# Turning pairs of bf16 as float32 words in the first stage of a recurrent-convolution and gated-unit gradient kernel

## The chip, the cores and the metric

The kernel runs on one core of a Trainium2 chip. The metric is the device time of one launch in microseconds (us). The engines are named as the profile does: PE is TensorE's matmul, PEld its weight load, DVE is VectorE, ACT is ScalarE, POOL is GpSimd, SP is SyncE, which here only issues DMAs.

## The reference

The function takes q, k, v (each 2048 rows of 1024, bf16), a four-tap filter shift_k, a long filter ssm_k (1024 channels of 2048 taps), a skip weight ssm_D, and three matrices w_gate, w_up (1024 x 3584) and w_down (3584 x 1024). It returns the output and the gradient of every input for a given grad_out.

```
xn = layernorm(q)
s  = xn * (long_conv(shift_conv(k) * v) + kv * ssm_D)     # long_conv by FFT of length 4096, kv = shift_conv(k) * v
h  = (xn @ w_gate) * (xn @ w_up)                          # 2048 x 3584
g  = silu(h @ w_down)
out = q + s * g
return out, grads of (q, k, v, shift_k, ssm_k, ssm_D, w_gate, w_up, w_down)
```

## The kernel before

**Stages.** The first stage (to about 513 us) computes the two products xn @ w_gate and xn @ w_up, forms h, and beside it runs the forward part of the long convolution. The second computes bm = h @ w_down and the gates (to about 710 us). The later ones compute the gradients; nothing of the change is in them but the names of a few views.

**The first stage on PE.** The 3584 columns are cut into 14 slabs of 256 columns of each of the two matrices (`load_slab`, tile `wslab`). A unit of work (`gu_unit`) takes one slab and four blocks of 128 rows (one, two or four blocks in the beginning). For each block eight matmuls of 512 columns sum over the 1024 channels: stationary is a 128x128 piece of the transposed normalized rows `XNT`, moving is the slab (L656). ACT copies the result to `gut` (L658), DVE forms `hN` = gate * up, POOL's queue stores it to `Hd`, and later the block is transposed ("turned") by PE to `hT`, since the second stage needs h with the 3584 columns in partitions. A turn is a matmul in transpose mode with the data as stationary operand and a 128x128 identity as moving operand; it goes to PSUM (tile `tr`), and ACT copies it out (L691). The turn of a unit is queued (`defer`) and done five blocks later (`flush(5)`).

The normalized rows are turned the same way, eight 128x128 pieces for a block of 128 rows, in `layer_norm` (L597, L608) and, for the last eight blocks, in `turn_late` (L617).

**The convolution.** Channels are worked in eight slices of 128 (`ds`). The transform of length 4096 over the rows is done as small DFTs: PE multiplies the rows of one residue (row number modulo 8) by tables of sines and cosines (`cmm`, L235), and DVE combines the residues (helper `tt` at L213 and `stt` at L284). There are two forms. With eight residues (`fwd8`) PE runs 16 matmuls of 256 columns and DVE combines more; with four (`fwd4_half`, `fwd4_sums`, `fwd4_outs`) PE runs 32 and DVE combines less. The list `EIGHT` names the pairs (slice, kind) that take the eight-residue form; kind 0 is the filter's spectrum in slices 1 to 7, kind 1 the data's (in slice 0 the other way round). The filter's 2048 taps of 128 channels are turned by `h_rows`: two blocks of eight turns (L752, L754), each of the elements 8 apart in a row.

**What sets the order.** The convolution is a generator that yields after each step with the step's cost on DVE in us, from which 0.95 of the PE time inside it (`pe_us`) is taken off (`net`). A planner (`make_pump`) lets it run so far that the costs done stand to their total `F_TOTAL` as the blocks of work done on PE stand to `NT` (225). The order that comes out is fixed on every engine. At the end of the stage PE goes on with matmuls of the second stage (`bm_first`, `late_mm`), and the four steps of the last inverse transform are put behind fixed ones of them:

```
    at = (52, 55, 58, 61)
    for n in range(at[3] + 1):
        mm = late_mm(n)
        if n in at:
            with tc.issue_after(mm.ins):
                step()
```

Of the kernel before, what the change touches and what calls it, by code (L numbers as in the profile page):

```python
# [10 lines left out]
ACT = mybir.ActivationFunctionType  # L11
ALU = mybir.AluOpType
AX = mybir.AxisListType
BF16 = mybir.dt.bfloat16
# [5 lines left out]
def build_kernel(  # L20
# [87 lines left out]
    KFd = dram.tile([8, P, 16, 256], BF16, name="KFd")  # L108
    DYFd = dram.tile([8, P, 16, 256], BF16, name="DYFd")
    GUd = dram.tile([NSL, 2, P, 2, 8, SLW], BF16, name="GUd")  # L110
    Hd = dram.tile([NSL, P, 2, NB, P], BF16, name="Hd")
    HTd = [[dram.tile([4, P, n, 256], BF16, name=f"HTd{i}{j}") for j, n in enumerate((8, 8, 8, 4))] for i in range(2)]
    DGd = dram.tile([NSL, 2, S, SLW], BF16, name="DGd")


    const = ctx.enter_context(tc.tile_pool(name="const", bufs=1))
    ident = const.tile([P, P], BF16, name="ident")
    make_identity(nc, ident[:])
    mhpi = const.tile([P, 1], F32, name="mhpi")
    nc.vector.memset(mhpi[:], -np.pi / 2)  # L120
    negpi = const.tile([P, 1], F32, name="negpi")
# [64 lines left out]
    def turn_tables(psp):  # L186

        for j in range(2):
            for rq in range(2):
                ps = psp.tile([P, 4, 2, P], BF16, name="psY")  # L190
                for i in range(4):
                    for k in range(2):
                        nc.tensor.transpose(ps[:, i, k, :], T4[j][:, 4 * rq + i, k, :], ident[:])
                nc.scalar.copy(out=TI[:, j, 4 * rq:4 * rq + 4], in_=ps[:])
                yield

# [15 lines left out]
    def tt(o, a, b, op):  # L212
        pinned(V.tensor_tensor(o, a, b, op))  # L213
# [315 lines left out]

    def keep_busy(n):  # L530
        for i in range(n):
            mm = nc.tensor.matmul(busy[:, i % 4, :], ident[:], ident[:], start=True, stop=True)
        return mm

    keep_busy(58)
# [11 lines left out]
    def load_slab(sl, eng):  # L547
        w = fw.tile([P, DC, 2, SLW], BF16, name="wslab")
        fs = slice(sl * SLW, (sl + 1) * SLW)
        for a, wsrc in ((0, B_w_up), (1, B_w_gate)):  # L550
            last = eng.dma_start(out=w[:, :, a, :], in_=wsrc[:, fs].rearrange("(dc p) f -> p dc f", p=P))
        return w, last

    def ln_load(b0, n, x4):
# [6 lines left out]

    tr_ln, act_copy = [None], [None]
    turn_rows = []

    def layer_norm(b0, n, x4):
        def small(name, dt=F32):
# [21 lines left out]
        for i in range(n):  # L588
            b = b0 + i
            q, qi = divmod(b, 4)  # L590
            last = V.tensor_scalar(x4[:, i, :], x4[:, i, :], mv[:, i, 0:1], RSTD[:, b:b + 1], op0=SUB, op1=MUL)
            if b < 2:
                for hh in range(2):
                    ps = ps_st.tile([P, 4, P], BF16, name="tr")
                    for dc in range(4):
                        d0 = (4 * hh + dc) * P
                        tr_ln[0] = nc.tensor.transpose(ps[:, dc, :], x4[:, i, d0:d0 + P], ident[:])  # L597
                    act_copy[0] = nc.scalar.copy(out=XNT[0][:, 4 * hh:4 * hh + 4, b * P:b * P + P], in_=ps[:])
                if b == 0:
                    with tc.issue_after(tr_ln[0].ins):  # L600
                        keep_busy(10)
                continue
            if b0 >= 8:
                turn_rows.append((x4[:, i, :], q, qi))
                continue
            ps = ps_st.tile([P, DC, P], BF16, name="tr")
            for dc in range(DC):
                tr_ln[0] = nc.tensor.transpose(ps[:, dc, :], x4[:, i, dc * P:(dc + 1) * P], ident[:])  # L608
            act_copy[0] = nc.scalar.copy(out=XNT[q][:, :, qi * P:(qi + 1) * P], in_=ps[:])
        c, r0 = divmod(b0, 8)  # L610
        return last, root, st(xnn[:, c, r0:r0 + n, :], x4[:, 0:n, :])

    def turn_late():
        for i, (x, q, qi) in enumerate(turn_rows):
            ps = ps_st.tile([P, DC, P], BF16, name="tr")
            for dc in range(DC):
                tr_ln[0] = nc.tensor.transpose(ps[:, dc, :], x[:, dc * P:(dc + 1) * P], ident[:])  # L617
            act_copy[0] = nc.scalar.copy(out=XNT[q][:, :, qi * P:(qi + 1) * P], in_=ps[:])
        turn_rows.clear()

    nop = lambda: None
# [18 lines left out]
    def gu_unit(sl, b0, n, w, tick):  # L640

        if n == 4:
            turn_of[0] += 1
            if turn_of[0] % 3 == 0 and sl < NSL - 2:
                gut = U[5][:, 2048:4096].rearrange("p (a i f) -> p a i f", a=2, i=4)
            else:
                gut = fg.tile([P, 2, 4, SLW], BF16, name="gut")
            hN = fg.tile([P, 2, 4, P], BF16, name="hN", bufs=3)
        else:
            gut = lnp.tile([P, 2, 2, SLW], BF16, name="gut_s", bufs=6)  # L650
            hN = lnp.tile([P, 2, 2, P], BF16, name="hN_s", bufs=6)
        for i in range(n):
            q, qi = divmod(b0 + i, 4)
            ps = ps_gu.tile([P, 512], F32, name="psg")
# [11 lines left out]

        def multiply():
            with tc.issue_after(last.ins) if b0 + n <= 4 and chunk[0] <= 2 else nullcontext():
                by_half = lambda t: t.rearrange("p i (a f) -> p a i f", a=2)
                tt(hN[:, :, 0:n], by_half(gut[:, 0, 0:n]), by_half(gut[:, 1, 0:n]), MUL)  # L670
            st(Hd[sl][:, :, b0:b0 + n, :], hN[:, :, 0:n])
            defer(turn)
        hn[0] = multiply

# [8 lines left out]

        def turn():
            hT = fg.tile([P, 2, 2, 2, P], BF16, name="hT") if chunk[0] > 5 else lnp.tile([P, 2, 2, 2, P], BF16, name="hT_s", bufs=5)
            ps = ps_tr.tile([P, 2, 2, 2, P], BF16, name="tr")
            for a in range(2):
                for i in range(n):
                    nc.tensor.transpose(ps[:, i // 2, a, i % 2, :], hN[:, a, i, :], ident[:])
            if n == 4:  # L690
                nc.scalar.copy(out=hT[:], in_=ps[:])  # L691
            else:
                nc.scalar.copy(out=hT[:, 0, :, 0:n], in_=ps[:, 0, :, 0:n])
            store(hT)

    h_out = []
    ht_st = [None]
    EIGHT = ((0, 0), (0, 1), (5, 0), (6, 0), (7, 0), (7, 1))
    INV8 = (2, 4, 5, 6, 7)
    SHIFT_W = 8 * 2.3  # L700

# [4 lines left out]
    def conv_forward():  # L706
# [36 lines left out]
        def h_rows(ds, c):  # L743
            if ds == 8:
                return
            hrow = S_["h", ds]
            if c == 0:
                S_["hx"] = cf.tile([P, NB, P], BF16, name="hx")
            pe_us[0] += 0.47
            ps = ps_tr.tile([P, 8, P], BF16, name="tr")  # L750
            with tc.issue_after(tr_ln[0].ins):
                nc.tensor.transpose(ps[:, 0, :], hrow[:, c, :, 0], ident[:])  # L752
            for r in range(1, 8):
                nc.tensor.transpose(ps[:, r, :], hrow[:, c, :, r], ident[:])  # L754
            nc.scalar.activation(S_["hx"][:, 8 * c:8 * c + 8, :], ps[:], ACT.Copy, scale=WSC)
            if c == 1:
                h_out.append(ds)
                if ds + 1 < 8:
                    load_h(ds + 1)
# [122 lines left out]
        cx.release()  # L882
        kst.release()

    F_TOTAL = 4 * SHIFT_W + 3.0 + 8 * (0.5 + FWD4_W + 1.3 + PROD_W + INV_W) + 10.0 - 0.95 * 8 * (4 * 1.75 + 0.95 + 4 * 0.9)
    F_TOTAL += len(EIGHT) * (FWD8_W - 9.6 + 0.95 * 1.75) - 2.0
    F_TOTAL += len(INV8) * (INV8_W - INV_W + 0.95 * 1.8)
    conv = conv_forward()
# [72 lines left out]
    slabs.append(w)  # L961

    def load_wd(j):
        return ld(WD[j], B_w_down[j * 512:(j + 1) * 512, :].rearrange("(c p) d -> p c d", p=P))

    def ht_rows(bp, f0, f1):
        assert f0 % 8 == 0 and f1 == min(f0 + 8, NF)
# [287 lines left out]
    def gate(b, ps, parts=None):  # L1255
# [23 lines left out]
        def turn():  # L1279
            ps = ps_tr.tile([P, DC, P], BF16, name=tr_name[0])  # L1280
            for dc in range(DC):
                nc.tensor.transpose(ps[:, dc, :], dbm[:, dc * P:(dc + 1) * P], ident[:])
            nc.scalar.copy(out=DBMT[b // 4][:, :, (b % 4) * P:(b % 4 + 1) * P], in_=ps[:])
        if b >= 12:
            defer(turn)
# [185 lines left out]
            next(others, None)  # L1471

    def load_h(sl):
        h = u8(HSL[sl % 3], "p (a b f) -> p a b f", a=2, b=NB)
        ld(h, Hd[sl])
        hs[sl] = h

# [60 lines left out]

    def dwd_mm(ps, h, f, dh):
        for b in range(NB):  # L1540
            nc.tensor.matmul(ps, h[:, f, b, :], DBM[b // 4][:, b % 4, dh * 512:(dh + 1) * 512],  # L1541
                             start=(b == 0), stop=(b == NB - 1))

    flush()
# [1 line left out]
    for k in range(NSL - 1):  # L1546
# [23 lines left out]
        for f in range(2):  # L1570
            if (k, f) == (12, 1):
                d_row = wo.tile([P, D], BF16, name="wbs")
                ps = ps_b.tile([P, 512], F32, name="psb")
                nc.tensor.matmul(ps[0:8, 0:P], ddo[:], ident[:], start=True, stop=True)
# [93 lines left out]
    for g in range(1, 4):  # L1668
        for b in (4 * g, 4 * g + 2):
            end = b == NB - 2  # L1670
            pss = [ps_x.tile([P, D], F32, name="psx") for i in range(2)]
            for n in range(12 if end else 14):
# [3 lines left out]
                    DBM[n] = u8((7, 0, 1, 9)[n], a=4)  # L1676
                    ld(DBM[n], DBMd[512 * n:512 * n + 512, :].rearrange("(b u) d -> u b d", u=P))
                if end and n == 4:
                    h = u8(2, "p (a b f) -> p a b f", a=2, b=NB)
# [87 lines left out]
```

## Time and profile before

| | us |
|---|---|
| three runs | 1917.39, 1917.96, 1918.56 |
| median | 1917.96 |
| span of the profiled execution | 1916.6 |
| PE busy | 1905.7 (99%) |
| DVE busy | 1557.1 (81%) |
| ACT busy | 640.0 (33%) |
| POOL busy | 334.5 (17%) |

The span runs from the first to the last instruction of one profiled execution, and the three timed runs took 0.8 to 2.0 us more than it. The granted clock of PE was 1.000 over the span. A row of a group of instructions reads: line, engine, operation, output<-inputs, shape, count | busy us, mean ns of one | idle time before them. A row in order of time reads: start, length, engine, line, operation, output<-inputs, count. The mean of a matmul is its latency; matmuls overlap, so the step from start to start is what one takes on PE.

### The profile page before, as it was taken

Reading aid. Unit: us, or ns where it says so; the run is one execution under the profiler, and the core shown is the slowest. Engines: PE = TensorE matmul, PEld = TensorE weight load, DVE = VectorE, ACT = ScalarE, POOL = GpSimd, SP = SyncE. Lnnn points to the kernel's source line nnn. Section 1 sums busy time; section 2 is a strip of 40 time slices with the busy share of each in tenths; the row PEclk is TensorE's granted clock in tenths of the full one; section 3 lists DMA queues with packets and bytes.
Section 4 is the critical chain, followed back from the end, with each engine's and each line's share of the span. In section 5 each row is a group of like instructions: output and inputs, shape, how many; then the busy total and the mean of one; then the engine's idle time right before and its main releaser. Section 6 shows DMA issues by size and latency. Waiting matters only on the chain. (4 is left out here: it accounts for less than half of the span.)

```text
span 1916.6 us, 27330 instructions
## 1 busy us (share of the span) xinstructions
PE 1905.7 (99%) x10915; PEld 1024.9 (53%) x10915; DVE 1557.1 (81%) x1723; ACT 640.0 (33%) x946; POOL 334.5 (17%) x465
## 2 busy tenths in 40 slices
PE   8999999999999999999999999999999999999999
PEld 5555555545544456666666665664444444444444
DVE  8999999999997556887999999999995205788862
ACT  5864555646433233432222222222222102011121
POOL 5121212111113220001031221111212101111120
PEclk9999999999999999999999999999999999999999
DMA  8776867668679997677887698585787999999962
GB/s 293 271 261 216 265 209 234 211 234 299 237 246 287 316 287 250 205 240 236 269 271 261 220 263 270 180 286 177 217 255 173 206 205 191 184 184 195 193 180 97
DMA packets 425487, 444.28 MB, mean 232 GB/s; under 512 B 268784, under 2 KB 343180, under 8 KB 410896
## 3 DMA queue, kind: packets, MB, share of 16 engines
q1 hardware_dynamic: 367888, 239.03, 46.9%
q0 software_dynamic: 41152, 174.15, 29.1%
q10 hardware_dynamic: 16320, 29.36, 4.1%
q8 instruction: 85, 1.39, 0.3%
q14 instruction: 42, 0.34, 0.1%
HBM read 193.87 MB, written 189.84 MB: 200 GB/s over the span
## 5 line engine op out<-in xcount | busy, mean ns | idle before, releaser
L656 PE MATMUL psg<-wslab,U 128*128 128x512 bf16 x1792 | 407.3, 379 | 3.0 <-DMA wslab<-in_B_w_gate_dram 2.0
L1458 PE MATMUL psb<-U,U 128*128 128x512 bf16 x1792 | 397.1, 379 | 0.0
L1603 PE MATMUL psx<-U,dgut 128*128 128x512 bf16 x1536 | 333.0, 379 | 0.5 <-DVE dxn L213 0.5
L1603 PEld LDWEIGHTS <-dgut 128*128 128x128 bf16 x1792 | 175.3, 98 | 212.1 <-issue 0.8
L1458 PEld LDWEIGHTS <-U 128*128 128x128 bf16 x1792 | 175.2, 98 | 198.0
L656 PEld LDWEIGHTS <-U 128*128 128x128 bf16 x1792 | 172.2, 98 | 187.4 <-issue 2.5
L1441 PE MATMUL psb<-wdt,U 128*128 128x256 bf16 x1792 | 205.6, 273 | 0.0
L213 DVE TENSOR_TENSOR W<-W 128x1024 f32<-128x1024 f32 (+1 forms) x192 | 189.1, 1001 | 4.2
L1441 PEld LDWEIGHTS <-U 128*128 128x128 bf16 x1792 | 175.3, 98 | 29.2
L1541 PE MATMUL psb<-U,U 128*128 128x512 bf16 x816 | 177.3, 379 | 0.0
L1463 ACT CAST wb<-psb 128x512 bf16<-128x512 f32 x112 | 65.6, 586 | 315.4 <-PE psb L1458 310.5
L1208 DVE SCALAR_TENSOR_TENSOR dkp<-dkT,kT 128x1024 bf16<-128x1024 bf16 (+2 forms) x64 | 78.3, 1224 | 104.0 <-DMA dkT<-DKSHd 102.2
L994 PE MATMUL psbm<-U,ht 128*128 128x512 bf16 x672 | 146.0, 379 | 0.0
L1541 PEld LDWEIGHTS <-U 128*128 128x128 bf16 x896 | 87.4, 98 | 104.3
L658 ACT CAST gut<-psg 128x512 bf16<-128x512 f32 x156 | 91.3, 588 | 120.0 <-PE psg L656 119.1
L1635 ACT ACTIVATE dx_t<-dxn 128x1024 bf16<-128x1024 f32 x15 | 15.9, 1057 | 324.2 <-DVE dxn L213 320.3
L994 PEld LDWEIGHTS <-ht 128*128 128x128 bf16 x672 | 65.6, 98 | 78.0
L213 DVE TENSOR_TENSOR U<-U,dht 128x2048 bf16<-128x2048 bf16 x56 | 68.3, 1221 | 46.4 <-ACT dht L1443 46.4
L1443 ACT CAST dht<-psb 128x512 bf16<-128x512 f32 x112 | 65.6, 587 | 116.3 <-PE psb L1441 116.3
L66 POOL DMA_DIRECT2D Hd<-hN x54 | 37.1, 686 | 292.3 <-DVE hN L213 289.4
L1582 ACT CAST wbs<-psb 128x512 bf16<-128x512 f32 x51 | 29.9, 586 | 145.4 <-PE psb L1541 137.3
L213 DVE TENSOR_TENSOR W<-SP 128x1024 f32<-128x1024 f32 x64 | 74.5, 1219 | 2.5 <-ACT SP L296 1.7
(261 smaller groups left out, 2386.3 us busy)
## 6 DMA issues: line engine op xcount, KB each, us to landing
U<-GUd SPq DMA_DIRECT2D x28, 1024.0 KB, 8.7
DGd<-U SPq DMA_DIRECT2D x28, 1024.0 KB, 6.5
GUd<-gut ACTq DMA_DIRECT2D x39, 512.0 KB, 5.5
out_dram<-wb SPq DMA_DIRECT2D x112, 128.0 KB, 4.8
U<-Hd SPq DMA_DIRECT2D x14, 1024.0 KB, 5.9
Hd<-hN POOLq DMA_DIRECT2D x54, 256.0 KB, 4.2
HTd<-hT SPq DMA_DIRECT2D x52, 256.0 KB, 3.9
ht<-HTd SPq DMA_DIRECT2D x18, 512.0 KB, 7.7
```

The lines of the kernel that those rows point to most:

```text
L66: ins = nc.gpsimd.dma_start(out=out, in_=in_)
L213: pinned(V.tensor_tensor(o, a, b, op))
L656: gu_mm[0] = nc.tensor.matmul(ps[:], XNT[q][:, dc, qi * P:(qi + 1) * P], w[:, dc].rearrange("p a f -> p (a f)"), start=(dc == 0), stop=(dc ...
L658: nc.scalar.copy(out=gut[:, :, i], in_=ps[:].rearrange("p (a f) -> p a f", a=2))
L994: mm = nc.tensor.matmul(ps[:, dh * 512:(dh + 1) * 512], ht(fc)[:, i * P:(i + 1) * P], WD[fc // 4][:, fc % 4, dh * 512:(dh + 1) * 512], sta ...
L1208: ins = V.scalar_tensor_tensor(prod[:].rearrange("p r d -> p (r d)")[:, lo:H], dkT[:, 0, lo:H], 1.0, kT[:, 0, 13 + m + lo:13 + m + H], op0 ...
L1441: nc.tensor.matmul(ps[:, x * SLW:(x + 1) * SLW], DBMT[2 * hf + g][:, dc, (b % 4) * P:(b % 4 + 1) * P], wdt[:, dc, :], start=(dc == 0), sto ...
L1443: nc.scalar.copy(out=dht[:, 2 * e:2 * e + 2].rearrange("p b f -> p (b f)"), in_=ps[:])
L1458: nc.tensor.matmul(ps[:], XN[b // 4][:, b % 4, dc * P:(dc + 1) * P], dgus[b // 8][:, :, b % 8], start=(b == 0), stop=(b == NB - 1))
L1463: nc.scalar.copy(out=wb[:, dc % 2].rearrange("p a f -> p (a f)"), in_=ps[:])
L1541: nc.tensor.matmul(ps, h[:, f, b, :], DBM[b // 4][:, b % 4, dh * 512:(dh + 1) * 512], start=(b == 0), stop=(b == NB - 1))
L1603: nc.tensor.matmul(ps[:, dh * 512:(dh + 1) * 512], t[n][:, f, i * P:(i + 1) * P], WGU[n][:, f, dh * 512:(dh + 1) * 512], start=(n == 0 and ...
```

## The change

A 32-bit word of two neighbouring bf16 is turned as one float32. One turn moves 128 rows of 128 words, which is 256 bf16 columns, to 128 partitions, and each partition then holds two bf16 rows interleaved; ACT's copy parts them. Half as many turns are issued for h (4 instead of 8 for four blocks), for the normalized rows and for the filter rows. Since a partition now holds neighbouring columns, other things follow that order: channel 8p + m instead of 128m + p for XNT and the slabs, the row pairs of w_down, and `Hd` in natural order. The identity becomes float32, and the bf16 identity is a view of every second half-word of it. Two entries of `EIGHT`, (5, 0) and (6, 0), go back to four residues. The planner's numbers follow.

```diff
-    Hd = dram.tile([NSL, P, 2, NB, P], BF16, name="Hd")
+    Hd = dram.tile([NSL, P, NB, SLW], BF16, name="Hd")
...
-    ident = const.tile([P, P], BF16, name="ident")
-    make_identity(nc, ident[:])
+    ident4 = const.tile([P, P], F32, name="ident4")
+    make_identity(nc, ident4[:])
+    ident = ident4[:].bitcast(BF16).rearrange("p (c j) -> p j c", j=2)[:, 1]
...
-            last = eng.dma_start(out=w[:, :, a, :], in_=wsrc[:, fs].rearrange("(dc p) f -> p dc f", p=P))
+            last = eng.dma_start(out=w[:, :, a, :], in_=wsrc[:, fs].rearrange("(p m) f -> p m f", m=DC))
...
+    def turn_x(x, q, qi, c0, n):
+
+        ps = ps_st.tile([P, n, P], F32, name="tr")
+        for c in range(n):
+            tr_ln[0] = nc.tensor.transpose(ps[:, c, :], x.bitcast(F32).rearrange("p (w i) -> p w i", i=4)[:, :, c0 + c], ident4[:])
+        act_copy[0] = nc.scalar.copy(out=XNT[q][:, 2 * c0:2 * (c0 + n), qi * P:(qi + 1) * P].rearrange("p (c j) s -> p c j s", j=2),
+                                     in_=ps[:].bitcast(BF16).rearrange("p c (s j) -> p c j s", j=2))
...
                 for hh in range(2):
-                    ps = ps_st.tile([P, 4, P], BF16, name="tr")
-                    for dc in range(4):
-                        d0 = (4 * hh + dc) * P
-                        tr_ln[0] = nc.tensor.transpose(ps[:, dc, :], x4[:, i, d0:d0 + P], ident[:])
-                    act_copy[0] = nc.scalar.copy(out=XNT[0][:, 4 * hh:4 * hh + 4, b * P:b * P + P], in_=ps[:])
+                    turn_x(x4[:, i], 0, b, 2 * hh, 2)
...
-            ps = ps_st.tile([P, DC, P], BF16, name="tr")
-            for dc in range(DC):
-                tr_ln[0] = nc.tensor.transpose(ps[:, dc, :], x4[:, i, dc * P:(dc + 1) * P], ident[:])
-            act_copy[0] = nc.scalar.copy(out=XNT[q][:, :, qi * P:(qi + 1) * P], in_=ps[:])
+            turn_x(x4[:, i], q, qi, 0, 4)
...
-                by_half = lambda t: t.rearrange("p i (a f) -> p a i f", a=2)
-                tt(hN[:, :, 0:n], by_half(gut[:, 0, 0:n]), by_half(gut[:, 1, 0:n]), MUL)
-            st(Hd[sl][:, :, b0:b0 + n, :], hN[:, :, 0:n])
+                tt(hN[:, 0:n], gut[:, 0, 0:n], gut[:, 1, 0:n], MUL)
+            st(Hd[sl][:, b0:b0 + n, :], hN[:, 0:n])
...
-            ps = ps_tr.tile([P, 2, 2, 2, P], BF16, name="tr")
-            for a in range(2):
-                for i in range(n):
-                    nc.tensor.transpose(ps[:, i // 2, a, i % 2, :], hN[:, a, i, :], ident[:])
+            ps = ps_tr.tile([P, 2, 2, P], F32, name="tr")
+            for i in range(n):
+                nc.tensor.transpose(ps[:, i // 2, i % 2, :], hN[:, i, :].bitcast(F32), ident4[:])
+            halves = ps[:].rearrange("f q i s -> f q (i s)").bitcast(BF16).rearrange("f q (i s a) -> f q a i s", i=2, a=2)
             if n == 4:
-                nc.scalar.copy(out=hT[:], in_=ps[:])
+                nc.scalar.copy(out=hT[:], in_=halves)
...
-    EIGHT = ((0, 0), (0, 1), (5, 0), (6, 0), (7, 0), (7, 1))
+    EIGHT = ((0, 0), (0, 1), (7, 0), (7, 1))
...
-            pe_us[0] += 0.47
-            ps = ps_tr.tile([P, 8, P], BF16, name="tr")
+            pe_us[0] += 0.25
+            ps = ps_tr.tile([P, 4, P], F32, name="tr")
+            pairs = hrow[:, c].rearrange("p u r -> p (u r)").bitcast(F32).rearrange("p (u i) -> p u i", i=4)
             with tc.issue_after(tr_ln[0].ins):
-                nc.tensor.transpose(ps[:, 0, :], hrow[:, c, :, 0], ident[:])
-            for r in range(1, 8):
-                nc.tensor.transpose(ps[:, r, :], hrow[:, c, :, r], ident[:])
-            nc.scalar.activation(S_["hx"][:, 8 * c:8 * c + 8, :], ps[:], ACT.Copy, scale=WSC)
+                nc.tensor.transpose(ps[:, 0, :], pairs[:, :, 0], ident4[:])
+            for i in range(1, 4):
+                nc.tensor.transpose(ps[:, i, :], pairs[:, :, i], ident4[:])
+            nc.scalar.activation(S_["hx"][:, 8 * c:8 * c + 8, :].rearrange("u (i j) d -> u i j d", j=2),
+                                 ps[:].bitcast(BF16).rearrange("u i (d j) -> u i j d", j=2), ACT.Copy, scale=WSC)
...
-    F_TOTAL = 4 * SHIFT_W + 3.0 + 8 * (0.5 + FWD4_W + 1.3 + PROD_W + INV_W) + 10.0 - 0.95 * 8 * (4 * 1.75 + 0.95 + 4 * 0.9)
+    F_TOTAL = 4 * SHIFT_W + 3.0 + 8 * (0.5 + FWD4_W + 1.3 + PROD_W + INV_W) + 10.0 - 0.95 * 8 * (4 * 1.75 + 0.5 + 4 * 0.9)
...
-        return ld(WD[j], B_w_down[j * 512:(j + 1) * 512, :].rearrange("(c p) d -> p c d", p=P))
+        return ld(WD[j].rearrange("p (s a) d -> p s a d", a=2), B_w_down[j * 512:(j + 1) * 512, :].rearrange("(s p a) d -> p s a d", s=2, a=2))
...
-            nc.tensor.matmul(ps, h[:, f, b, :], DBM[b // 4][:, b % 4, dh * 512:(dh + 1) * 512],
+            nc.tensor.matmul(ps, h[:, b, f * P:(f + 1) * P], DBM[b // 4][:, b % 4, dh * 512:(dh + 1) * 512],
```

The uses of the identity that stay bf16 (the tables, the rows of dbm, PE's warm-up in `keep_busy`) take the view.

More of the change, by code (lines that the diff above doesn't have):

```diff
@@ L192, in turn_tables @@
                     for k in range(2):
-                        nc.tensor.transpose(ps[:, i, k, :], T4[j][:, 4 * rq + i, k, :], ident[:])
+                        nc.tensor.transpose(ps[:, i, k, :], T4[j][:, 4 * rq + i, k, :], ident)
                 nc.scalar.copy(out=TI[:, j, 4 * rq:4 * rq + 4], in_=ps[:])
@@ L531, in keep_busy @@
         for i in range(n):
-            mm = nc.tensor.matmul(busy[:, i % 4, :], ident[:], ident[:], start=True, stop=True)
+            mm = nc.tensor.matmul(busy[:, i % 4, :], ident, ident, start=True, stop=True)
         return mm
@@ L613, in turn_late @@
     def turn_late():
[L614 to L618, printed above, removed]
+        for x, q, qi in turn_rows:
+            turn_x(x, q, qi, 0, 4)
         turn_rows.clear()
@@ L647, in gu_unit @@
                 gut = fg.tile([P, 2, 4, SLW], BF16, name="gut")
-            hN = fg.tile([P, 2, 4, P], BF16, name="hN", bufs=3)
+            hN = fg.tile([P, 4, SLW], BF16, name="hN", bufs=3)
         else:
             gut = lnp.tile([P, 2, 2, SLW], BF16, name="gut_s", bufs=6)
-            hN = lnp.tile([P, 2, 2, P], BF16, name="hN_s", bufs=6)
+            hN = lnp.tile([P, 2, SLW], BF16, name="hN_s", bufs=6)
         for i in range(n):
@@ L685, in turn @@
             hT = fg.tile([P, 2, 2, 2, P], BF16, name="hT") if chunk[0] > 5 else lnp.tile([P, 2, 2, 2, P], BF16, name="hT_s", bufs=5)
-            ps = ps_tr.tile([P, 2, 2, 2, P], BF16, name="tr")
-            for a in range(2):
-                for i in range(n):
-                    nc.tensor.transpose(ps[:, i // 2, a, i % 2, :], hN[:, a, i, :], ident[:])
+            ps = ps_tr.tile([P, 2, 2, P], F32, name="tr")
+            for i in range(n):
+                nc.tensor.transpose(ps[:, i // 2, i % 2, :], hN[:, i, :].bitcast(F32), ident4[:])
+            halves = ps[:].rearrange("f q i s -> f q (i s)").bitcast(BF16).rearrange("f q (i s a) -> f q a i s", i=2, a=2)
             if n == 4:
-                nc.scalar.copy(out=hT[:], in_=ps[:])
+                nc.scalar.copy(out=hT[:], in_=halves)
             else:
-                nc.scalar.copy(out=hT[:, 0, :, 0:n], in_=ps[:, 0, :, 0:n])
+                nc.scalar.copy(out=hT[:, 0, :, 0:n], in_=halves[:, 0, :, 0:n])
             store(hT)
@@ L1281, in turn @@
             for dc in range(DC):
-                nc.tensor.transpose(ps[:, dc, :], dbm[:, dc * P:(dc + 1) * P], ident[:])
+                nc.tensor.transpose(ps[:, dc, :], dbm[:, dc * P:(dc + 1) * P], ident)
             nc.scalar.copy(out=DBMT[b // 4][:, :, (b % 4) * P:(b % 4 + 1) * P], in_=ps[:])
@@ L1473, in load_h @@
     def load_h(sl):
-        h = u8(HSL[sl % 3], "p (a b f) -> p a b f", a=2, b=NB)
+        h = u8(HSL[sl % 3], "p (b f) -> p b f", b=NB)
         ld(h, Hd[sl])
@@ L1573, in build_kernel @@
                 ps = ps_b.tile([P, 512], F32, name="psb")
-                nc.tensor.matmul(ps[0:8, 0:P], ddo[:], ident[:], start=True, stop=True)
+                nc.tensor.matmul(ps[0:8, 0:P], ddo[:], ident, start=True, stop=True)
                 nc.scalar.copy(out=d_row[0:8, 0:P], in_=ps[0:8, 0:P])
@@ L1678, in build_kernel @@
                 if end and n == 4:
-                    h = u8(2, "p (a b f) -> p a b f", a=2, b=NB)
+                    h = u8(2, "p (b f) -> p b f", b=NB)
                     ld(h, Hd[NSL - 1])
```

## The prediction

> **What bounds the kernel now.** I read the page's table of engines first, then the busy time by stretches of 48 us, then who waited for whom, then the order of time at the places that the change touches.
>
> ```profile
> PE 1905.7 (99%) x10915; PEld 1024.9 (53%) x10915; DVE 1557.1 (81%) x1723; ACT 640.0 (33%) x946; POOL 334.5 (17%) x465
> ...
> DVE  8999999999997556887999999999995205788862
> ```
> The first line says that TensorE (PE) works all the time: 1916.6 - 1905.7 leaves 10.9 us of idle time in the whole span. The second says that VectorE (DVE) is as full as PE in the first 12 slices (to 575 us). The change lies inside that stretch. The answer by stretches (columns: window, its length, then busy us and instructions of PE, PEld, DVE, ACT, POOL):
>
> ```profile
> 96.00:144.00 48.00, 47.91 (x318) 28.09 (x315) 47.55 (x49) 29.40 (x40) 11.98 (x17) 1.00 0.79 260
> ...
> 624.00:672.00 48.00, 48.00 (x224) 21.80 (x223) 25.18 (x40) 12.06 (x12) 10.17 (x16) 1.00 1.08 315
> ```
> In the first stage PE and DVE are both full; afterwards PE alone. The list of waits agrees: PE waited 6.5 us in the whole span, all but 0.5 of it in the first 50 us. So a microsecond taken from PE in the first stage is worth a microsecond only if DVE gives one up too, or has room. How much room it has is seen where the stage ends: PE runs matmuls of the next stage (psbm) until the last inverse transform (psY<-HX) needs what DVE finishes last (HX, L284). In order of time, PE then DVE:
>
> ```profile
> 550.78 5.99 PE L994 MATMUL psbm<-U,U 128*128 128x512 bf16 x27
> 556.61 0.60 PE L446 MATMUL psY<-HX,TI 128*128 128x256 bf16 x4
> ...
> 552.59 2.49 DVE L284 SCALAR_TENSOR_TENSOR HX<-W 128x512 bf16<-128x512 f32 x4
> ```
> DVE is done at 552.59 + 2.49 = 555.1, PE asks at 556.6. DVE has 1.5 us of room at this join, and at the last turn of h some 0.5 us (hN ready at 512.4, its matmul at 513.2, held by the copy of the turn before).
>
> **What the transposes cost now.** The groups by line give their counts:
>
> ```profile
> L689 PE MATMUL tr<-ident,hN 128*128 128x128 bf16 x432 | 33.1, 219 | 0.1
> ...
> L754 PE MATMUL tr<-ident,U 128*128 128x128 bf16 x112 | 9.6, 226 | 0.0
> ...
> L689 PEld LDWEIGHTS <-hN 128*128 128x128 bf16 x432 | 28.7, 98 | 12.1 <-issue 0.3
> ...
> L754 PEld LDWEIGHTS <-U 128*128 128x128 bf16 x112 | 8.2, 147 | 3.0 <-issue 2.8
> ```
> The mean of 219 ns is a latency, not a price, as matmuls overlap. The price is the step from one start to the next, read from the order of time:
>
> ```profile
> 206.19 0.22 PE L752 MATMUL tr<-ident,U 128*128 128x128 bf16 x1
> 206.25 0.60 PE L754 MATMUL tr<-ident,U 128*128 128x128 bf16 x7
> 206.69 1.04 PE L457 MATMUL psY<-HX,TI 128*128 128x256 bf16 x8
> ...
> 208.46 1.67 PE L656 MATMUL psg<-wslab,U 128*128 128x512 bf16 x7
> 209.97 0.61 PE L689 MATMUL tr<-ident,hN 128*128 128x128 bf16 x8
> 210.41 0.81 PE L656 MATMUL psg<-wslab,U 128*128 128x512 bf16 x3
> ```
> Eight turns of h hold PE from 209.97 to 210.41: 0.44 us, 55 ns each. Eight of the filter rows, whose elements lie 16 bytes apart in SBUF, take 206.19 to 206.69: 62.5 ns each; their weight loads are the slower ones (147 against 98 ns). Normalized rows, 32 turns at 25.67 in 1.99 us: (1.99 - 0.22) / 31 = 57 ns. The same reading gives (1.67 - 0.38) / 6 = 215 to 216 ns for a 512-column matmul and, from the 16 forward-transform matmuls that took 1.91 us at 226.85, (1.91 - 0.27) / 15 = 109 ns for one of 256 columns.
>
> **The change, part by part.** *Removed:* 448 turns of h (432 + 16 in the smaller tile hN_s) x 55 ns = 24.6 us; 128 of normalized rows (16 + 16 + 32 + 64 at L597, L608, L617) x 57 = 7.3; 128 of filter rows (112 + 16) x 62.5 = 8.0. Together 39.9 us of PE.
>
> *Added:* half as many, 352, each of 128x128 float32. No row of this trace has a float32 operand on PE, so I bound one. Below: 55 ns, the bf16 turn, if only the count of columns matters. Above: 216 ns, the 512-column row, if four bytes make four passes. I take 62.5 ns, because the nearest row is the filter's: there the load already fetches 128 elements one by one with no two neighbours together, which is the most a float32 load of 128 words must do, and the matmul behind it still streams 128 columns. 352 x 62.5 = 22.0 us. The filter and normalized rows keep a 16-byte pitch, the h rows become contiguous words.
>
> The Trainium skill speaks against this: "TensorE: Matmul & The Clock Gate", sections "LDWEIGHTS (loading the stationary operand)" and "Weight-path perf modes — Fast Weight Load (FWL) and DoubleRow", says that the fast weight load is off for FP32 and that a plain load takes columns / 1.2 ns, 107 ns for 128 columns. The sum by the page would be, as an estimate, 352 x 107 = 37.7 us added. No row here shows a plain load of 128 columns, so the trace neither agrees nor disagrees.
>
> *Two transforms back to four residues* (the filter spectra of slices 5 and 6): each needs 32 instead of 16 matmuls of 256 columns, so 32 x 109 ns = 3.5 us more on PE. On DVE they get shorter. From the order of time: the eight-residue one of slice 6 runs from 434.87 to 451.39, less 0.60 for an hN product inside, 15.9 us; the four-residue one at 374.16 to 383.96, less 0.61, 9.2 us. Two save 13.4 us. ACT copies the same four SP tiles either way.
>
> *The sum.* PE: 39.9 - 22.0 - 3.5 = 14.4 us less. DVE: 13.4 us less, plus its 1.5 us of room, plus what it gains at the beginning, where it waited 0.9 us for the last turn at L617 and 1.7 us for an SP copy, both behind PE. So DVE allows 14.9 to 17.5 us, PE's 14.4 binds, narrowly. The planner's total F_TOTAL falls by 15.5 of 441 (3.4 up for the turns, 18.9 down for the two transforms) and is spread over the same 225 ticks, so both engines thin out along the whole stage, though PE's gain is even and DVE's falls on two slices. Before slice 5 PE can be a few us ahead; hN products have five units (5 x 8 x 216 ns = 8.6 us) between product and turn to take that up.
>
> *Copies behind the turns.* ACT reads 1024 halves interleaved in words instead of 1024 in a row. Rows near it: 1.02 us for 1024 bf16 (L691) and 1.03 for 1024 float32 (L296): the count decides, so I take 1.02. If it doubled, filter blocks, which follow one another through one PSUM buffer, would wait 1 us in each of 8 pairs: 8 us; below, nothing.
>
> *Costed at nothing.* The h product keeps 1024 elements (0.68 us, as contiguous gate products have). The h store becomes half as many, longer pieces; POOL is 5 to 13 us busy in 48 and h is not read back before 1253.8. Wd pieces grow from 2 to 4 KB; slab pieces stay 512 bytes. A slab is asked for a whole slab ahead (some 35 us of PE), and its two halves land after 5.4 and 8.1 us; were that cover gone, a wait like the 1.0 us at the start would come 12 times. The float32 identity is written by POOL before PE's warm-up, and read with a stride by it; I put 0.3 us (0 to 1) there, of which the wait for the first slab (1.0 us at 9.3) hides some. Nothing waits anew elsewhere: both engines enter the second stage earlier by about the same, where DVE has 23 us idle in 48.
>
> So about 14 us come off the span: 1916.6 - 14.0 = 1902.6. The three runs took 0.8 to 2.0 us more than the profiled span, their median 1917.96 is 1.4 above it; **forecast 1904.0 us**.
>
> **Rivals.** *A, the plain load binds:* if a float32 weight is fed as two bf16 wide, a turn lasts like 256 columns, 109 ns. Then 352 x 109 = 38.4, PE: 39.9 - 38.4 - 3.5 = 2.0 us more, 1920. Against it: the slowed load of the filter rows (147 ns) still let the stream go at 62.5. For it: in that row only the pitch was bad, not the width. By the skill's 107 ns the estimate is 1.3 us more, no change that could be seen.
>
> *B, several passes (the other side):* each turn streams its columns more than twice, at L689, L754 and turn_x. At four passes, 216 ns, 352 x 216 = 76.0, so 39.9 - 76.0 - 3.5 = 39.6 us more: 1957.6. It breaks even at (39.9 - 3.5) / 352 = 103 ns and is slower by over 0.2% from 114 ns. For it: twice the bytes per column and no float32 matmul in this trace. Against it: a turn moves words, it does not need the product split. The skill's page ("Terms") says that transpose mode makes FP32 four times faster on this chip, which would exclude it; no run shown so far bears that out.
>
> *C, DVE caps it:* at 55 ns PE would save 39.9 - 19.4 - 3.5 = 17.0 us and DVE's 14.9 to 17.5 decides: 1901 to 1903.
>
> *D, half the gain:* 80 ns each (28.2 us, 8.2 saved), or the copies doubled (14 - 8 = 6 saved): 1910 to 1912.
>
> **How the numbers follow.** Chances: forecast and C together 0.56, D 0.10, A 0.14, B and anything past 114 ns 0.20. A difference below 0.2% (3.8 us) is about what a measurement of this kernel can't tell from no change. So faster 0.66 (forecast, C, D), same 0.14 (A), slower 0.20. The range runs from C's 1901 to just past A, 1922, which leaves out B's far part, below 2 in 10. The likeliest case alone: 1901 to 1907.
>
> **What would show it.** Right: 352 float32 turns, with 4 of h between two 512-column matmuls in about 0.25 us (0.44 in A, 0.86 in B); the psY<-HX matmul of the join at about 542.5, with no PE wait above 1 us there; DVE's L284 group smaller by 8 instructions; L691 near 1.02 us; the stage after unchanged in length. Wrong: a step above 100 ns between turns, PE waiting for DVE at L446 or L689, or ACT's copies near 2 us.

## The result and the profile after

The changed kernel took 1920.75 us in the median (20 runs, 1920.53 to 1923.23), the kernel before 1917.75 in the same comparison (20 runs). The ratio is 1.0016, 95% interval 1.0009 to 1.0022: 3.0 us longer, inside the 0.2% that the prediction counted as no change, though the interval lies above 1. The forecast was 1904.0. The span of the profiled execution is 1919.1 us (1916.6 before), the granted clock of PE 1.0.

The page of the changed kernel, its table of engines and DVE's row of 40 slices:

```profile
PE 1902.0 (99%) x10465; PEld 1029.3 (54%) x10595; DVE 1544.8 (80%) x1699; ACT 640.0 (33%) x946; POOL 327.0 (17%) x465
...
DVE  8999999999987555887899999999996205788862
```

The 10595 weight loads are the planned count: 10915 - 352 + 32. (130 matmul records are missing from this trace, so PE's busy time reads a little low.) DVE gave up 12.3 us. Its 9s now end one slice earlier, but the stage did not get shorter. By stretches of the changed kernel (window, length, busy us and instructions of PE, PEld, DVE, ACT, POOL):

```profile
96.00:144.00 48.00, 47.74 (x278) 27.87 (x283) 47.45 (x49) 28.79 (x39) 11.83 (x18) 1.00 0.77 259
...
432.00:480.00 48.00, 47.44 (x270) 27.28 (x274) 44.77 (x45) 28.51 (x41) 4.94 (x8) 1.00 0.84 286
...
624.00:672.00 48.00, 47.79 (x220) 21.79 (x223) 25.53 (x40) 11.72 (x13) 10.18 (x16) 1.00 1.06 299
```

PE is as full as before in each. DVE has 3 us idle at 432 to 480, where slices 5 and 6 were meant to free it. The same is seen at the join of the stages, in order of time, PE then DVE:

```profile
559.84 0.60 PE L447 MATMUL psY<-HX,TI 128*128 128x256 bf16 x4
...
551.12 2.50 DVE L285 SCALAR_TENSOR_TENSOR HX<-W 128x512 bf16<-128x512 f32 x4
```

DVE is done at 553.6, PE asks at 559.8. DVE's room grew from 1.5 to 6.2 us, and PE came 3.2 us later instead of 14 us earlier. The stage after has its old length: its successor (psb<-wdt, L1441) starts at 709.29, 3.25 later than before.

So it is PE, and the term to look at is the float32 turn. Groups of the changed kernel, then order of time:

```profile
L686 PE MATMUL tr<-ident,hN 128*128 128x128 f32 x216 | 32.7, 273 | 0.2
...
L753 PE MATMUL tr<-ident,U 128*128 128x128 f32 x48 | 8.4, 284 | 0.0
...
L686 PEld LDWEIGHTS tr<-ident,hN 128*128 128x128 f32 x216 | 26.8, 141 | 10.7 <-ACT hT L689 0.8
...
L753 PEld LDWEIGHTS tr<-ident,U 128*128 128x128 f32 x48 | 7.2, 209 | 0.2
```

```profile
200.81 0.60 PE L686 MATMUL tr<-ident,hN 128*128 128x128 f32 x4
201.24 0.38 PE L236 MATMUL psF<-hx,TF 128*128 128x256 bf16 x2
...
211.52 0.52 PE L753 MATMUL tr<-ident,U 128*128 128x128 f32 x3
211.88 1.04 PE L458 MATMUL psY<-HX,TI 128*128 128x256 bf16 x8
...
25.96 2.20 PE L570 MATMUL tr<-ident,U 128*128 128x128 f32 x16 [0.92 <-DVE U L600]
```

Four turns of h hold PE from 200.81 to 201.24: 0.43 / 4 = 108 ns each. The last three of four filter turns take 211.52 to 211.88, 120 ns each. Sixteen of normalized rows, also of words 16 bytes apart, take (2.20 - 0.28) / 15 = 128 ns each. Half as many turns at twice the step give nothing back. The latencies (273 and 284 ns) are close to the 272 of a 256-column bf16 matmul, not to the 219 of the bf16 turn.

### The profile page after: what moved, and what is told of

It reads as the page before. It is cut to its first block, busy times and chain, and to the rows that moved or that the text cites. A ratio compares the mean times of both kernels' runs of the same rounds, so it can differ in the third digit from the quotient of the medians.

```text
span 1919.1 us, 26552 instructions
## 1 busy us (share of the span) xinstructions
PE 1902.0 (99%) x10465; PEld 1029.3 (54%) x10595; DVE 1544.8 (80%) x1699; ACT 640.0 (33%) x946; POOL 327.0 (17%) x465
## 4 chain that ended last, share of the span: by engine, by line
PE 97%; ACT 1%; issue 1%; DVE 1%; DMA 1%; SPq 0%; ACTq 0%
PE psb L1458 20%; PE psx L1603 20%; PE psg L655 19%; PE psb L1441 10%; PE psbm L994 10%; PE psb L1541 9%; PE psF L236 3%; PE tr L686 1%; PE psY L447 1%; PE psY L1152 1%; PE psx L1541 1%; DMA wslab<-in_B_w_gate_dram 1%; PE psY L458 0%; PE tr L570 0%; ACT SP L258 0%
## 5 line engine op out<-in xcount | busy, mean ns | idle before, releaser
L655 PE MATMUL psg<-wslab,U 128*128 128x512 bf16 x1738 | 401.5, 379 | 6.1 <-DMA wslab<-in_B_w_gate_dram 2.6
L1441 PE MATMUL psb<-wdt,U 128*128 128x256 bf16 x1792 | 205.6, 273 | 0.0
L1441 PEld LDWEIGHTS <-U 128*128 128x128 bf16 x1792 | 175.3, 98 | 29.2
L214 DVE TENSOR_TENSOR W<-W 128x1024 f32<-128x1024 f32 (+1 forms) x186 | 184.0, 1006 | 4.1
L66 POOL DMA_DIRECT2D Hd<-hN x54 | 30.3, 562 | 296.0 <-DVE hN L214 283.3
```

Of the source, the lines that this page charges most:

```text
L655: gu_mm[0] = nc.tensor.matmul(ps[:], XNT[q][:, dc, qi * P:(qi + 1) * P], w[:, dc].rearrange("p a f -> p (a f)"), start=(dc == 0), stop=(dc ...
L1441: nc.tensor.matmul(ps[:, x * SLW:(x + 1) * SLW], DBMT[2 * hf + g][:, dc, (b % 4) * P:(b % 4 + 1) * P], wdt[:, dc, :], start=(dc == 0), sto ...
```

## The experiments

**1. The step of a turn by itself (steps).** Ten rows of 32 matmuls behind the warm-up of the changed kernel, whose output stays as it is. They differ in type, pitch and width; a row's first operand is stationary, its second moving, and the data in `Dz` are zeros. The kernel took 1952.97 us (one run), 32 us more than the changed kernel where some 25 were expected; only its rows are read.

```diff
+    for i in range(N):
+        nc.tensor.transpose(bh[:, i % 8, :], Dz[:, 0:128], ident)
...
+    for i in range(N):
+        nc.tensor.transpose(bh[0:127, i % 8, :], Dz[:, 0:127], ident)
...
+    for i in range(N):
+        nc.tensor.transpose(busy[:, i % 4, :], Dz[:, 0:256].bitcast(F32), ident4[:])
...
+    for i in range(N):
+        nc.tensor.transpose(busy[:, i % 4, :], fw_[:, :, i % 4], ident4[:])
...
+    for i in range(N):
+        nc.tensor.transpose(busy[0:64, i % 4, :], Dz[:, 0:128].bitcast(F32), ident4[:])
...
+    for i in range(N):
+        nc.tensor.transpose(busy[:, i % 4, 0:64], Dz[0:64, 0:256].bitcast(F32), ident4[0:64, 0:64])
```

> The changed kernel with ten rows of 32 matmuls put behind the warm-up, each row with its own line, four 512-column matmuls between rows; their output is not used, and the kernel is some 25 us longer for them. Read is the step from start to start in each row. Two theories of what makes a float32 turn take 109 ns contiguous and 128 ns at a 16-byte pitch. Theory L (the load binds): the weight load of 128 words is the longer part. Then a float32 turn with 64 weight columns falls to about 55 to 65 ns, one with all 128 weight columns but only 64 moving columns (64 rows) stays near 109, and a bf16 turn with 127 weight columns, if the short load needs all 128, rises from 55 towards 100. Theory M (the moving side binds): the float32 identity streams at half the rate of a bf16 one, 128 columns like 256. Then 64 weight columns leave 109, and 64 moving columns give about 55 (or the load's own time, if that is longer). In both the 16-byte pitch at 128 ns is a load that has become longer than the stream. bf16 contiguous 55 to 57, bf16 at a 16-byte pitch 62, bf16 matmul of 256 columns 109.

In order of time in that kernel: start, length, and a shape that gives stationary and moving size:

```profile
6.90 2.01 PE L552 MATMUL tr<-ident,Dz 128*128 128x128 bf16 x32
...
9.61 2.19 PE L555 MATMUL tr<-ident,Dz 128*128 128x128 bf16 x32
...
12.50 2.06 PE L558 MATMUL tr<-ident,Dz 128*127 128x128 bf16 x32
...
18.25 1.13 PE L564 MATMUL tr<-ident,Dz 64*128 64x64 bf16 x32
...
20.18 3.66 PE L567 MATMUL tr<-ident,Dz 128*128 128x128 f32 x32
...
24.54 3.99 PE L570 MATMUL tr<-ident,Dz 128*128 128x128 f32 x32
...
29.23 3.66 PE L573 MATMUL tr<-ident,Dz 128*64 128x128 f32 x32
...
33.68 2.20 PE L576 MATMUL tr<-ident,Dz 64*128 64x64 f32 x32
...
36.69 3.66 PE L579 MATMUL tr<-Dz,ident 128*128 128x256 bf16 x32
```

The step is (length - one latency) / 31; the latencies are the groups' means, 189 to 283 ns. The bf16 turn (L552) takes 57.8 ns, the float32 turn (L567) 109.3, and the bf16 matmul with 256 moving columns (L579) 109.3 too. Halving the stationary columns of the float32 turn (L573) leaves it at 109.3; halving the moving ones, with the partitions (L576), gives 63.7, where the bf16 turn of that size (L564) takes 30.4. So the step goes with the moving columns and not with the stationary ones, as Theory M had it: 128 float32 columns pass like 256 bf16 columns. The size of the output does not set it either: L579 writes twice as many float32 values as L567 in the same step. In every float32 row both operands are float32, so these rows do not tell whether the type of the moving operand or that of the weights makes the pass twice as long.

The weight loads of the same rows show that the load isn't what holds the contiguous turn:

```profile
L570 PEld LDWEIGHTS tr<-ident,Dz 128*128 128x128 f32 x32 | 4.0, 208 | 0.1
...
L567 PEld LDWEIGHTS tr<-ident,Dz 128*128 128x128 f32 x32 | 3.6, 141 | 0.2
L573 PEld LDWEIGHTS tr<-ident,Dz 128*64 128x64 f32 x32 | 3.5, 111 | 0.2
...
L555 PEld LDWEIGHTS <-Dz 128*128 128x128 bf16 x32 | 2.2, 145 | 0.2
L576 PEld LDWEIGHTS tr<-ident,Dz 64*128 64x128 f32 x32 | 2.1, 139 | 0.4 <-issue 0.4
L558 PEld LDWEIGHTS <-Dz 128*127 128x127 bf16 x32 | 2.0, 138 | 0.2
L552 PEld LDWEIGHTS <-Dz 128*128 128x128 bf16 x32 | 1.9, 96 | 0.2
```

With a load of 111 instead of 141 ns (L573, L567) the step stays at 109.3. Loads of 139 and 138 ns stand behind steps of 63.7 and 59.3 ns (L576, L558): a load of this length is hidden, or nearly so. Rows that load elements 16 bytes apart are slower: 63.4 ns for bf16 (L555, load 145) where 57.8 are contiguous, and 119.6 for float32 (L570, load 208) where 109.3 are. The last is the filter's case in the changed kernel, where 120 was read above. Why the normalized rows, at the same pitch, took 128 there was not looked into.

The Trainium skill, "TensorE: Matmul & The Clock Gate", section "Weight-path perf modes — Fast Weight Load (FWL) and DoubleRow", says that the fast load needs 128 weights of a type other than FP32; the trace agrees, 138 and 141 ns without it against 96 with it (L558, L567, L552). The rule of that page's section "LDWEIGHTS (loading the stationary operand)", columns / 1.2, gives 107 ns for 128 columns as an estimate. That is near the measured step, but by coincidence: with 64 columns the rule's estimate halves to 53 ns, and the step stayed at 109.3 (L573).

**2. The turns alone (turns_only).** The changed kernel with the two transforms left at eight residues.

```diff
-    EIGHT = ((0, 0), (0, 1), (7, 0), (7, 1))
+    EIGHT = ((0, 0), (0, 1), (5, 0), (6, 0), (7, 0), (7, 1))
```

> The change without its last part: float32 turns and their orders, but slices 5 and 6 keep eight residues. Theory T (a float32 turn costs what two bf16 turns cost, and the 3 us of the result are the two transforms): PE gets 224 x 108 ns + 64 x 128 + 64 x 120 = 40.1 us for the 39.9 removed, so 1917.7, within 1 us of the kernel before. Rival W (the turns themselves lose, by new waits behind ACT's copies or at the start): 1920 to 1921, as the whole change.

Measured: 1918.40 us (11 runs), ratio 1.0004, interval 0.9995 to 1.0013. Its join is at 556.68 (556.61 before), its L1441 starts at 706.14 (706.04 before). That is Theory T: against the 1917.48 us of the kernel before in that comparison the turns as float32 cost 0.9 us, which the interval does not tell from nothing. Rival W's 3 us are not there.

**3. The transforms alone (residues_only).** The kernel before with that line of `EIGHT` changed the other way, as the change has it.

> The kernel before with slices 5 and 6 back to four residues, bf16 turns kept. Theory T: PE gets 32 matmuls of 256 columns more, 32 x 109 ns = 3.5 us, DVE 13.4 us less that nobody waits for: 1921.2, and DVE reaches the end of its forward part some us ahead of PE. Rival W: no change, 1917.8. Rival V (DVE was the bound of the first stage): faster, down to 1917.8 - 13.4 + 3.5 = 1908.

Measured: 1920.90 us (11 runs), ratio 1.0018, interval 1.0009 to 1.0027: 3.4 us more than the kernel before in that comparison, where 32 x 109 ns = 3.5 were expected (Theory T; Rival W had none, Rival V a gain of 10). The group of the forward transform in it, which had 192 matmuls and 23.7 us before:

```profile
L235 PE MATMUL psF<-kv,TF 128*128 128x256 bf16 x224 | 27.2, 273 | 0.1
```

DVE's relief of 13.4 us turns into idle time: its wait for gate and up copies (hN<-gut) rises from 1.1 to 6.3 us, and at the join it is done 7.1 us before PE asks (1.5 before). DVE alone does not hold this stage.

**4. The turns of h alone (h_only).** The kernel before with `ident4`, the natural order of `Hd`, the row pairs of w_down and float32 turns of h; normalized rows, filter rows and `EIGHT` as before.

```diff
-            ps = ps_tr.tile([P, 2, 2, 2, P], BF16, name="tr")
-            for a in range(2):
-                for i in range(n):
-                    nc.tensor.transpose(ps[:, i // 2, a, i % 2, :], hN[:, a, i, :], ident[:])
+            ps = ps_tr.tile([P, 2, 2, P], F32, name="tr")
+            for i in range(n):
+                nc.tensor.transpose(ps[:, i // 2, i % 2, :], hN[:, i, :].bitcast(F32), ident4[:])
```

> The kernel before with float32 turns for h alone, the contiguous ones; normalized and filter rows stay bf16, six entries of EIGHT. The version that the measured steps point to: 224 x 108.5 ns = 24.3 us for 448 x 55 = 24.6 us, so 0.3 us less on PE and POOL's h stores 0.13 us shorter each: 1917.4 to 1917.9, not to be told from the kernel before. If a float32 turn of h had some price beside its step (a wait of its copy, a change between types on PE), 54 units would show it: 0.1 us each is 5 us, 1923.

Measured: 1917.52 us (11 runs; before on that chip 1917.47), ratio 1.0, interval 0.9991 to 1.0009. Changing between the two types on PE has no price that this can show.

**5. One engine less, or both (lean_before, lean_after).** Is the two-engine sum of the prediction sound? From both kernels the same 54 matmuls of 512 columns are left out, 54 x 216 ns = 11.7 us of PE.

```diff
+            nd = DC - 1 if n == 4 and i == 3 else DC
-            for dc in range(DC):
+            for dc in range(nd):
...
```

> The kernel before with 54 matmuls of 512 columns left out of xn @ w (the last of the eight sums for the fourth block of each full unit; so those blocks of h lack an eighth of their sum): 54 x 216 ns = 11.7 us less on PE, spread over the first stage as evenly as the turns are, DVE as before. It puts the saving that the prediction hoped for on PE without any change of DVE. Theory C (DVE is full in the first stage and has 1.5 us of room): the kernel gets 1.5 to 4 us faster, 1914 to 1916, and PE waits the rest, some 8 to 10 us, for DVE in the first stage or at the psY matmul behind it. Rival P (PE alone is the bound): the whole 11.7 us, 1905.8.

> The same 54 matmuls left out of the changed kernel, where DVE has 13.4 us less to do. Theory C: now DVE has the room, all 11.7 us come off the 1920.75 of the changed kernel: 1909, and PE waits at most 1 to 2 us more than in it. With lean_before this would say that the prediction's sum of the two engines was sound and only the price of a float32 turn was not. Rival P: also 1909, but then lean_before is at 1905.8, 3 us below it. Rival D (the order of work, not DVE's total, makes PE wait): 1912 to 1916.

Measured: lean_before 1916.80 us (10 runs), ratio 0.9993, interval 0.9984 to 1.0002; lean_after 1909.71 (4 runs), ratio to the kernel before 0.9959, interval 0.9943 to 0.9974. The kernel before keeps 0.7 of 11.7 us, less than Theory C's 1.5 to 4 and far from Rival P's 11.7. The changed one keeps 11.0 of 11.7 (1920.75 - 1909.71; these two stem from different comparisons, and by the ratios to the kernel before it is 7.8 + 3.0 = 10.8). What lean_before waits for on PE, the last turn of h, and a stretch of it:

```profile
PE psF L235 <- DVE kv L213: 3.6, 3, 2.5
...
PE psF L235 <- ACT SP L257: 2.0, 2, 1.0
PE psF L235 <- ACT SP L296: 1.6, 2, 1.3
PE tr L690 <- DVE hN L213: 1.5, 1, 1.5
```

```profile
512.51 0.62 PE L690 MATMUL tr<-ident,hN 128*128 128x128 bf16 x8 [1.48 <-DVE hN L213]
```

```profile
288.00:336.00 48.00, 44.91 (x292) 26.69 (x297) 47.55 (x39) 26.87 (x37) 11.07 (x16) 1.00 0.68 233
```

The same stretch of lean_after:

```profile
288.00:336.00 48.00, 47.74 (x282) 28.46 (x286) 47.23 (x39) 28.53 (x41) 8.65 (x14) 1.00 0.67 227
```

Without the transforms' relief PE stands idle for 3 us in 48 beside a full DVE (in the kernel before PE was 47.96 us busy there); with it PE stays full. DVE starts the last product hN at 511.77 us in lean_before and at 511.76 in the kernel before, and its turn comes at 512.51 instead of 513.21. These 0.7 us are all that came off: DVE's room that counts is the one at the last turn of h, not the 1.5 us at the join. So a saving on PE did need the two transforms' relief of DVE (with the planner's lower total that goes with it), and with it 11.7 us would have counted nearly whole.

**6. One transform more at eight residues (seven_eight, nt224).** If DVE's room at the join is real, DVE can be loaded until it ends last there. The first kernel gives slice 4 eight residues as well and sets `NT` to 219, six below the 225 of the kernel before, though its expectation says 224. The second, nt224, is the kernel before with `NT` at 224 and nothing else. It shows what one tick does and is not a full control for the six of seven_eight.

```diff
-    EIGHT = ((0, 0), (0, 1), (5, 0), (6, 0), (7, 0), (7, 1))
+    EIGHT = ((0, 0), (0, 1), (4, 0), (5, 0), (6, 0), (7, 0), (7, 1))
-    NT = 24 * 8.0 + 33
+    NT = 24 * 8.0 + 27
```

> The kernel before with one transform more in eight residues, the filter of slice 4, and the planner's ticks 224 instead of 225. PE has 16 matmuls less (1.7 us), DVE 6.7 us more. Theory J (the join after the first stage has 1.5 us of room): DVE ends at 555.1 + 6.7 = 561.8, PE asks at 556.6 - 1.7 = 554.9, waits 7 us there or in pieces before, and the kernel takes about 5 us more, 1923. Rival P (PE alone is the bound, DVE's lag is absorbed by the matmuls of the next stage): 1.7 us less, 1916.

> The control for seven_eight: the kernel before with the planner's ticks 224 instead of 225 and nothing else. If the 18 us of seven_eight came from its order, some of them show here (over 3 us); if they came from DVE's 6.7 us more and from what that does to the order, nothing does: 1917.5 within 2 us.

Measured: seven_eight 1935.57 us (4 runs), ratio 1.0094, interval 1.008 to 1.0107, a miss for both theories (1923 and 1916 us); nt224 1920.49 (10 runs), ratio 1.0013, interval 1.0004 to 1.0022, which is 3.0 us longer. Its expectation allowed 2 us if the order alone had no price, so it has one. In order of time in seven_eight:

```profile
531.07 1.03 PE L689 MATMUL tr<-ident,hN 128*128 128x128 bf16 x8 [3.69 <-DVE hN L213]
...
576.59 0.60 PE L446 MATMUL psY<-HX,TI 128*128 128x256 bf16 x4
```

PE loses its time ahead of the last turn of h (at 513.21 before), not at the join: there DVE is done at 563.9 and PE asks 12.7 us later. DVE starts the last product hN at 530.33, 18.6 us later than before (511.76); in nt224 it starts at 513.85, 2.1 us later. The last turns come 17.9 and 1.4 us later, in both cases the delay of the product less the 0.7 us of room that lean_before showed.

Where the 18.6 us come from can be estimated with the planner's formula in the kernel. At the last block of the stage it asks for 391.0 us of planned work in the kernel before, 392.7 in nt224 and 409.6 in seven_eight: 1.6 and 18.6 us more. With 224 ticks seven_eight would ask for 10.0 us more, so by this estimate some 8.6 of the 18.6 come from the lower `NT`. No kernel with seven transforms and 224 ticks was run, so this split is not shown.

Behind the last turn the matmuls stand in a fixed order, so room at the join cannot take up a delay inside the stage. PE took 45.5 us from the last turn to the join, where the kernel before took 43.4; its granted clock was 0.93 from 528 to 576 us (1.00 before).

**7. A third engine (pool_h, pool_h8, pool_h10).** With PE and DVE both full, the h products of whole units were moved to POOL, then also two and four more transforms to eight residues, each of which saves PE 16 matmuls and loads DVE by 6.7 us. This was the attempt at a version better than both.

```diff
-                tt(hN[:, :, 0:n], by_half(gut[:, 0, 0:n]), by_half(gut[:, 1, 0:n]), MUL)
+                (nc.gpsimd.tensor_tensor if chunk[0] > 5 and n == 4 else tt)(hN[:, :, 0:n], by_half(gut[:, 0, 0:n]), by_half(gut[:, 1, 0:n]), MUL)
```

> The kernel before with the products hN of the full units formed by GpSimd instead of DVE from the seventh chunk on. lean_before and lean_after say that PE's time counts only where DVE has room; here DVE gets room without PE getting work. DVE has some 50 x 0.60 = 30 us less. Theory C: PE is then the only bound and its work is unchanged, so 1917.5 less at most the 1 us that PE waits for DVE now. Rival S (GpSimd's product disturbs DVE or comes so late that h's turns wait): slower, 1920 or more, with DVE operations longer than 1.22 and 0.68 us or PE waiting at tr<-hN.

> As pool_h, and DVE's room is used: the filters of slices 3 and 4 take eight residues too (the planner's total 2.0 up so that the order fits). PE has 2 x 16 x 109 ns = 3.5 us less, DVE 13.4 more of its 30. Theory C: 1914. Rival S: slower than the kernel before.

> As pool_h8 with the filters of slices 1 and 2 as well (planner's total 4.0 up). PE 4 x 16 x 109 ns = 7.0 us less, DVE 26.9 more of its 30. Theory C: 1910.5, if the last 3 us of room are enough, else some us more. Rival S: slower than the kernel before.

Measured: 1988.57, 2002.33 and 2019.57 us; ratios 1.0368 (1.035 to 1.0387), 1.0453 (1.0423 to 1.0483), 1.0532 (1.0513 to 1.055). In order of time in pool_h:

```profile
303.15 1.23 DVE L213 TENSOR_TENSOR m<-m,KX 128x2048 bf16<-128x2048 bf16 x1
...
304.72 2.90 POOL L670 TENSOR_TENSOR hN<-U 128x1024 bf16<-128x1024 bf16 x1 [4.08 <-ACT U L658]
305.67 3.03 DVE L213 TENSOR_TENSOR m<-m,KX 128x2048 bf16<-128x2048 bf16 x1
```

The product takes 2.9 us here (2.7 in the mean of 51; on DVE 0.68), and the DVE instruction that starts inside it takes 3.03 us instead of 1.23. It ends at 308.70, 1.08 us after POOL's end at 307.62: as if it had begun when POOL was through. The Trainium skill, "SBUF — State Buffer", section "Who interferes with whom", says that a DVE instruction with two SBUF inputs contends with a GpSimd instruction that reads SBUF, and that the ports the two share are an exclusive lock in which issue order decides who blocks; this trace agrees, with the 3.03 us of a DVE product of two SBUF inputs.

The sum over the whole span says the same. The page of pool_h:

```profile
PE 1916.4 (96%) x10781; PEld 1030.0 (52%) x10915; DVE 1626.6 (82%) x1672; ACT 640.1 (32%) x946; POOL 471.6 (24%) x516
```

51 products left DVE, 51 x 0.68 = 35 us, and yet its busy time rose by 69.5 us (1557.1 before), so its other instructions took some 104 us longer. The kernel got 70.9 us longer. The next two transforms cost 13.8 us with 13.7 more on DVE, the last two 17.2 with 18.6 more. So Rival S held in all three. PE's granted clock was 0.95 from 60 to 640 us in pool_h (1.00 before); what part of PE's loss that is was not separated. No complete kernel tried beats the kernel before; h_only equals it.

## Why the prediction was wrong, point by point

**The step that failed** is the term "352 x 62.5 = 22.0 us". Measured: 224 turns of h (216 + 8) at 108 ns = 24.2 us, 64 of normalized rows at 128 = 8.2, 64 of filter rows at 120 = 7.7, together 40.1. With the other terms as they were, the sum is 39.9 - 40.1 - 3.5 = 3.7 us more instead of 14.4 less; measured were 3.0 more. This one price carries the whole miss. The value was taken from the filter's bf16 row, because its load is the hardest of the trace, and "the matmul behind it still streams 128 columns" was assumed for float32. The load was the wrong side: for the turns of h it is hidden, and the 128 columns count as 256 (steps). The rows 16 bytes apart take 10 to 19 ns more than that.

**Rival A had the number** (109 ns, 1920 us) by another mechanism than its own, which is luck: it let the load bind. In steps the step stayed at 109.3 ns when half the stationary columns were left out and the load fell from 141 to 111 ns. Its remark that a float32 weight may count as two is neither shown nor excluded, as no row has float32 on one side only. Its price held for the turns of h; the rows 16 bytes apart cost 120 to 128. Rival B's four passes (216 ns) are excluded by 108 ns. The Trainium skill, "TensorE: Matmul & The Clock Gate", section "Terms", says that transpose mode is four times faster for FP32; no run here shows it, since none has a float32 matmul without transpose mode.

**What held.** The removed 39.9 us: turns_only balances it against 40.1 within its interval. The transforms' 3.5 us on PE: 3.4 measured alone. DVE's 13.4: 12.3 fewer busy us over the span. That PE's gain needs DVE's, and would then count nearly whole: the lean pair, for 11.7 us. The 1.5 us of room that the sum gave DVE was read at the wrong place: at the last turn of h the lean pair and seven_eight show 0.7 (the prediction had read some 0.5 there), so DVE would have allowed from 14.1 us on instead of 14.9, just under the 14.4 of PE. ACT's copies of interleaved halves at 1.02 us: L689 of the changed kernel has a mean of 1018 ns. The identity's 0.3 us at the start did not appear: PE's wait for it is 1.4 us in both kernels. PE waited 2.6 instead of 2.0 us for slabs, all of it at the start, so the order of slabs costs at most 0.6 us. Rivals C and D had no place, since nothing was saved.

**What would have shown it** was named: 0.44 us for four turns of h meant A, and 0.43 was read.

## What to carry to other kernels

A row of the trace prices a new instruction form only by the side that binds it: ask separately what the load and what the matmul behind it would do, and measure the new form in a row of 32 before a change rests on it. Packing two elements into a wider word saves instructions, not time, where the wider word passes at half the rate. Where two engines are both full, test a saving by leaving work out of one of them: 0.7 or 11.0 us of the same 11.7 came through here, depending on the other.

## What was not expected of the hardware

- A float32 turn takes PE as long per moving column as two bf16 columns: 109.3 ns for 128 of the one and 256 of the other. Halving its stationary columns changes nothing.
- A weight load of 138 ns lies behind a step of 59.3 ns (57.8 with a load of 96); one of 208 ns, float32 words 16 bytes apart, goes with a step of 119.6 (109.3 contiguous).
- A DVE product begun inside one of POOL took 3.03 us instead of 1.23; moving 35 us of products from DVE to POOL raised DVE's busy time by 69.5 us.
- One tick in the planner's total put the last product hN 2.1 us later, and the kernel took 3.0 us more in the median.
